# Score bursts held until due, half chunks as 32-row slices and lent weight buffers in a hand-scheduled attention and SiLU block

## The chip, the cores and the metric

The kernel runs on one core of a Trainium2 chip. A core has five engines with queues of their own: TensorE (PE; its weight loads are shown apart as PEld), VectorE (DVE), ScalarE (ACT), GpSimd (POOL) and SyncE (SP, which issues nearly all DMAs here). The metric is the device time of one execution in microseconds, as the median of several runs. Times inside an execution come from one profiled execution, counted from its first instruction.

## The reference

A layer norm feeds multi-query attention (32 query heads of 20 columns, one key head, one value head) and a SiLU feed-forward block of width 1728; both are added to the input. S is 2048, D is 640, all in bfloat16.

```python
def _A_ref(x, wq, wk, wv, wo):
    q = (x @ wq).reshape(B, S, H, Dh).transpose(0, 2, 1, 3)
    k = x @ wk
    v = x @ wv
    scores = jnp.einsum("bhqd,bkd->bhqk", q, k) * (Dh ** -0.5)
    p = softmax(scores, axis=-1)
    o = jnp.einsum("bhqk,bkd->bhqd", p, v)
    return o.transpose(0, 2, 1, 3).reshape(B, S, H * Dh) @ wo
def _B_ref(x, w1, w2):
    return jnp.einsum("bsf,fd->bsd", silu(jnp.einsum("bsd,df->bsf", x, w1)), w2)
x = A_x
xn = layernorm(x)
return x + _A_ref(xn, A_wq, A_wk, A_wv, A_wo) + _B_ref(xn, B_w1, B_w2)
```

## The kernel before

Queries are cut into four chunks (QC) of 512 rows, heads into eight groups (NG) of four, so there are 32 head groups with 16 key tiles and four heads each: 2048 score blocks of 128 keys by 512 queries. A head has 20 columns padded to 32, so a score matmul uses 32 of TensorE's 128 rows, and up to four of them with different row groups run beside each other: a score burst. A value matmul uses 32 of the 128 columns and four of them make a quad; the weight products (projections, feed-forward, output) are cut into quads of the same kind. Going from bursts to quads or back is a switch of TensorE's tile shape.

There are eight PSUM banks. Bank 7 (UB) collects the value products of a group, the other seven hold scores and weight products in turn. A score block takes one of two ways:

- ScalarE takes the exponential of a set of two or three banks in one instruction (line 1140 of the kernel before).
- VectorE turns single banks into integers whose bits read as bfloat16 approximate the exponential (line 1336, "p1", into a z buffer, four heads to a batch). From each batch two shifted copies are made, on GpSimd (line 1375) or on VectorE (line 1380), and all three go through the value matmuls with different weights, so that the approximation's errors even out.

The order of the work is decided in Python when the kernel is built. A planner (class `Sched` and the loop at the end of `build`) keeps an estimated clock per engine, picks the next operation with `step_pe` or `step_other` and appends it to that engine's list; `emit` then writes the lists out with semaphore waits. On the chip each engine simply runs its list. `step_pe` collects candidates: "s" a score burst for ScalarE (`make_s_act`), "d" a score block for VectorE, "p" and "pd" value quads, "m" and "l" quads of weight products, "r" a 32-row slice of a weight chunk. It takes the first kind that can start, in an order that depends on TensorE's present shape. `row_slice` lets a whole weight chunk of 128 rows be done as four matmuls of 32 rows, each in a free row group of a score burst (issued by `row_mm`, line 441); `col_mm` (line 434) issues chunks as quads.

The constants of these choices are in `BASE`; the letters of `PLAN` name a rule out of `RULES` for each 10 us of planned time. `stay` is such a constant: if it is not 0, and TensorE is not in burst shape, and ScalarE has work in hand for longer than `stay` plus 230 ns, score bursts go nearly to the end of the order. `claim` opens VectorE's batches in z buffers that are idle; there are five, two of which share memory with a staging area of wq.

The feed-forward width 1728 is thirteen chunks of 128 rows and one of 64. The half chunks of two neighbouring query chunks are computed together (`h_pair`): the even one's 64 rows lie in the upper half of its chunk and the odd one's in the lower half, and the rest is zero. `ffn_mms` lists the fourteen chunks of an output tile in order. The output of the first three query chunks is made by `out_job`, that of the last one by `y_job` (feed-forward and the packs known so far), and `fin_job` with the last heads' part.

After the last exponential come, on TensorE, the last value quads, the row sums of the last group ("sum", line 973), the spread of their reciprocals (line 991) and the final chunks; VectorE adds them up (line 941) and two queues store the result. ScalarE copies the last value bank out in two halves (line 1237) ahead of the sums. Other lines that the text uses: 756 is the tanh of the SiLU, 618 a copy of the keys, 52 and 2 tanh instructions stand at lines 756 and 728, line 1648 is a filler matmul on zeros that the planner puts into gaps.

Of the kernel before, what the change touches and what calls it, by code (L numbers as in the profile page):

```python
# [14 lines left out]
P = 128  # L15
# [81 lines left out]
BASE = dict(hold2=0, bnd=4, pj=6000.0, rows=0, rowmin=3, lagmax=6, lagp=0, lagj=6, openlag=5, late=-0.02, lead=0.01, leadmax=0.02, need=460.0, hold=300.0, dwant=600.0, slack=550.0, dnow=400.0, hungry=0.0, patience=0.0, keep=460.0, open=2, zcap=9, stay=0.0, homes=1, want=1, claim=6)  # L97
RULES = dict(a={}, b=dict(keep=0.0), c=dict(lagp=3), d=dict(lagp=5), e=dict(lagp=0), f=dict(patience=200.0), g=dict(dwant=0.0),
             h=dict(zcap=4), i=dict(zcap=3), j=dict(homes=0), k=dict(leadmax=-1.0, lead=-1.0), l=dict(lead=0.08, leadmax=0.1),
             m=dict(need=560.0), n=dict(hold=0.0), o=dict(stay=460.0), p=dict(open=1), q=dict(slack=400.0), r=dict(hungry=1000.0), s=dict(claim=9), t=dict(open=3), u=dict(claim=4), v=dict(want=2), w=dict(slack=700.0), x=dict(hold2=4), y=dict(bnd=0), z=dict(pj=-1e9), A=dict(rows=0), B=dict(rows=2, rowmin=2), C=dict(pj=2000.0), D=dict(openlag=3), E=dict(pj=8000.0), F=dict(hold2=3), G=dict(rows=1))  # L100
PLAN = "aaanGtxBBExhEhmxadrBBzraCBBEGqtrztfFzrqhwnpofocotyxddmGjvmpBaBitntqo"
# [17 lines left out]
class Op:  # L119
    __slots__ = ("eng", "fn", "occ", "lat", "pre", "reads", "writes", "prio", "mode", "slots",  # L120
                 "start", "fin", "done", "deps", "inc", "job", "first", "last", "gate", "on_commit", "seq", "name",
                 "dma_sem", "dma_val", "port", "run", "cut", "ends", "sync")

    def __init__(self, eng, fn, occ, lat=0.0, pre=(), reads=(), writes=(), prio=5.0, mode=None, slots=None,
                 job=None, gate=None, on_commit=None, name=""):
        self.eng = eng
        self.fn = fn
        self.occ = occ
        self.lat = lat
        self.pre = list(pre)  # L130
        self.reads = list(reads)
        self.writes = list(writes)
        self.prio = prio
        self.mode = mode
# [12 lines left out]
        self.port = False  # L147
        self.cut = None
        self.sync = None
        self.ends = (True, True)  # L150
# [168 lines left out]
def build(nc, A_x, A_wq, A_wk, A_wv, A_wo, B_x, B_w1, B_w2, out, stack):  # L319
# [78 lines left out]
    z_t += [zx[:, i * HG * QW:(i + 1) * HG * QW] for i in range(2)]  # L398
    wq_st = zx[:, 0:DC * D].rearrange("p (c d) -> p c d", c=DC)
# [266 lines left out]
    def q_job(qc, k):  # L666
# [11 lines left out]
        xq_read[qc].append(job)  # L678
        op = Op("dve", lambda v: v.tensor_scalar_mul(q_st[:, st, :], bk(job.bank), QSCALE), t_dve(512), 140,  # L679
# [26 lines left out]
    xq_read = {k: [] for k in range(QC)}  # L706
    t_users = {}
    out_done = {}

    def h_pair(qb):  # L710
# [13 lines left out]
        for q in (qa, qb):  # L724
            xq_read[q].append(job.ops[-1])
        ts = (qb * FC + fk) % 2
# [16 lines left out]
    def h_job(qc, fk):  # L743
# [9 lines left out]
        xq_read[qc].append(job)  # L753
        ts = (qc * FC + fk) % 2
# [134 lines left out]
    def y_job(qc, i, hf):  # L889
        e0, e1 = hf * HALF, (hf + 1) * HALF  # L890
        mms = ffn_mms(qc, i, e0, e1, True, not YC[i]) + o_mms(qc, i, e0, e1, False, True, range(YC[i]))
        job = pe_job(f"y{qc}_{i}_{hf}", mms, (14 + YC[i]) * 140, dyn=True)
        op = Op("dve", lambda v: v.scalar_tensor_tensor(out=yx[:, i, e0:e1], in0=bk(job.bank, 0, HALF), scalar=0.5,  # L893
# [114 lines left out]
    att = {"sgroup": 0, "pgroup": 0, "n": 0, "items": 0, "value": 0.0}  # L1008
# [248 lines left out]

    def z_idle(k):
        b = z_last[k]
# [57 lines left out]
    def yx_users(zi):  # L1317
        return [wqp0] if zi >= NZ0 else []
# [213 lines left out]
    def ready_to_make(m):  # L1532
# [11 lines left out]
        if m[0] == "y":  # L1544
            if (m[1], m[2]) not in xres_op or any((m[1], fk) not in hc_op for fk in range(FC)):
                return False
            return all((m[1] - 1, t) in out_done for t in range(QTP)) and all((m[1], g) in pack_op for g in range((YC[m[2]] * P - 1) // (HG * DH) + 1))
# [105 lines left out]
    def pe_candidates():  # L1653
# [11 lines left out]
        lead = misc_done[0] / misc_total - PACE * prog - ENDLEAD * max(0.0, prog - ENDFROM) / (1.0 - ENDFROM)  # L1665
        behind = lead < ru.lead or recent() < BUSY
# [28 lines left out]
    def row_slice(piece):  # L1695

        job = piece.job
        if not job.dyn or not ru.rows or sc.pe_mode != "s" or sc.pe_set is None or sc.t["pe"] > sc.pe_set[2] + 1.0 or job.burst == sc.pe_set[0]:
            return None
        busy = sc.pe_set[1]  # L1700
        pick = next(((x, r) for x in job.rest for r in job.rest[x] if r not in busy), None)
        if pick is None and len(job.rest) < ru.rows and len(piece.mms) > ru.rowmin:
            x = next((x for x in list(piece.mms)[-2:0:-1] if x.cut is not None and all(p.done for p in x.pre)), None)
# [53 lines left out]
    def step_pe():  # L1757
# [34 lines left out]
        elif mode == "p":  # L1792
            order += ["p", "pd", "m", "d", "l"] if lag >= (ru.lagp if cur_job[0] is None else ru.lagj) else ["m", "pd", "p", "d", "l"]
# [35 lines left out]
    def commit_pe(e, op, what):  # L1829
# [244 lines left out]
```

## Time and profile before

| | |
|---|---|
| time, median of 3 runs | 693.72 us (693.70 to 693.74) |
| the profiled execution's own time | 693.9 us |
| its span, first to last instruction | 692.1 us |
| granted TensorE clock | 1.000 |
| busy on TensorE, ScalarE, GpSimd, VectorE | 680.5, 673.5, 593.0, 572.0 us |
| weight loads on TensorE | 229.7 us |
| chain that ended last | ScalarE 57%, TensorE 35%, VectorE 5%, GpSimd 3% |

In a row of groups stand the line, the engine and operation, what it writes and reads, the shapes and the count; then busy time and the mean duration in ns, and the engine's idle time before these instructions with what ended it. Rows of a timeline begin with the start and the length of a run of equal instructions, in us. Records of following instructions on one engine can overlap, since each lasts until its result has landed.

### The profile page before, as it was taken

To read this page: it belongs to the slowest core of one execution; us is meant where nothing else is said; L and a number is where in the kernel's file an instruction comes from. 1 tells how busy PE (TensorE), PEld (TensorE's weight loads), DVE (VectorE), ACT (ScalarE), POOL (GpSimd) and SP (SyncE) were. 2 spreads that over 40 slices of the span, in tenths; PEclk is the share of its full clock that TensorE was granted. 3 is DMA by queue.
4 is the path that set the end of the run, shared out by engine and by line. 5 is a ranking of instruction groups with operands and counts; after the bars stand their busy time and mean duration, and the time that the engine had idled before them with its cause. 6 is when DMAs were issued, how large, how long until landed. Compare 5 with 4: busy or idle time off the path is not lost.

```text
span 692.1 us, 22655 instructions
## 1 busy us (share of the span) xinstructions
PE 680.5 (98%) x9908; PEld 229.7 (33%) x9911; DVE 572.0 (83%) x977; ACT 673.5 (97%) x727; POOL 593.0 (86%) x355
## 2 busy tenths in 40 slices
PE   8999999999999999999999999999999999999998
PEld 5432222222222333322223333322222333333344
DVE  7788889988988788789989878789898877888843
ACT  6899999999999999999999999999999999999993
POOL 6658999899988789898998879989889999988890
PEclk9999999999999999999999999999999999999999
DMA  8642220222221222233202222122222202232201
GB/s 223 194 158 39 20 22 14 35 33 27 22 19 14 37 39 24 29 74 35 27 9 28 31 29 33 22 63 41 30 20 21 22 19 31 31 68 23 23 7 40
DMA packets 34241, 28.97 MB, mean 42 GB/s; under 512 B 15486, under 2 KB 29662, under 8 KB 34142
## 3 DMA queue, kind: packets, MB, share of 16 engines
q1 hardware_dynamic: 33854, 27.20, 25.5%
q8 instruction: 77, 1.26, 0.7%
q10 hardware_dynamic: 288, 0.33, 0.1%
q14 instruction: 22, 0.18, 0.1%
HBM read 11.09 MB, written 2.62 MB: 20 GB/s over the span
## 4 chain that ended last, share of the span: by engine, by line
ACT 57%; PE 35%; DVE 5%; POOL 3%; issue 1%; DMA 0%
ACT sbt L1140 53%; PE psall L434 11%; PE psall L1175 11%; PE psall L1052 11%; ACT sbt L756 3%; POOL sbt L1375 2%; DVE sbt L1336 1%; DVE sbt L552 1%; DVE sbt L550 1%; DVE sbt L594 1%; POOL sbt L836 0%; DMA sbt<-in_A_x_dram 0%; PE psall L608 0%; PE psall L973 0%; DVE sbt L679 0%
## 5 line engine op out<-in xcount | busy, mean ns | idle before, releaser
L1140 ACT ACTIVATE sbt<-psall 128x1024 bf16<-128x1024 f32 (+1 forms) x655 | 652.5, 1220 | 2.2 <-PE psall L1052 1.7
L1375 POOL TENSOR_SCALAR sbt<-sbt 128x2048 int16<-128x2048 int16 x279 | 530.5, 1901 | 62.7 <-DVE sbt L1380 12.7
L1336 DVE TENSOR_SCALAR sbt<-psall 128x512 int16<-128x512 f32 x656 | 428.8, 684 | 79.6 <-PE psall L1052 72.0
L1052 PE MATMUL psall<-sbt 32*128 32x512 bf16 x2048 | 265.9, 384 | 3.7 <-ACT sbt L1140 1.8
L1175 PE MATMUL psall<-sbt 128*32 128x512 bf16 x3360 | 267.7, 384 | 1.2 <-DVE sbt L1223 0.4
L434 PE MATMUL psall<-sbt 128*32 128x320 bf16 (+2 forms) x3844 | 226.6, 331 | 0.7 <-ACT sbt L1140 0.5
L1052 PEld LDWEIGHTS psall<-sbt 32*128 32x128 bf16 x2048 | 70.0, 91 | 248.8 <-ACT sbt L1140 194.9
L434 PEld LDWEIGHTS psall<-sbt 128*32 128x32 bf16 x3844 | 83.9, 95 | 77.7 <-issue 46.9
L1175 PEld LDWEIGHTS psall<-sbt 128*32 128x32 bf16 x3360 | 66.0, 94 | 115.1 <-issue 82.4
L836 POOL TENSOR_TENSOR sbt<-sbt 128x512 bf16<-128x512 f32 x30 | 38.3, 1276 | 6.8 <-DVE sbt L1380 4.8
L759 DVE SCALAR_TENSOR_TENSOR sbt<-sbt,psall 128x512 bf16<-128x512 bf16 x52 | 35.5, 683 | 5.6 <-ACT sbt L756 4.9
L1380 DVE TENSOR_SCALAR sbt<-sbt 128x2048 int16<-128x2048 int16 x49 | 39.8, 827 | 0.2
L756 ACT ACTIVATE sbt<-psall 128x512 bf16<-128x512 f32 x52 | 39.5, 760 | 0.0
L1223 DVE COPY sbt<-psall 128x512 f32<-128x512 f32 x31 | 21.1, 682 | 2.3 <-PE psall L1175 2.2
L441 PE MATMUL psall<-sbt 32*128 32x320 bf16 (+1 forms) x60 | 20.5, 342 | 0.1
L1648 PE MATMUL psall<-sbt 128*32 128x256 bf16 (+1 forms) x264 | 18.1, 370 | 1.2 <-DVE sbt L474 1.2
L878 DVE SCALAR_TENSOR_TENSOR sbt<-psall,sbt 128x320 bf16<-128x320 f32 x24 | 11.6, 483 | 3.7 <-PE psall L434 2.6
L679 DVE TENSOR_SCALAR sbt<-psall 128x512 bf16<-128x512 f32 x20 | 13.5, 674 | 0.1
L893 DVE SCALAR_TENSOR_TENSOR sbt<-psall,sbt 128x320 f32<-128x320 f32 x8 | 3.9, 485 | 9.8 <-PE psall L434 9.7
L572 POOL TENSOR_SCALAR sbt<-sbt 128x640 bf16<-128x640 bf16 x12 | 10.4, 878 | 1.5 <-DVE sbt L564 1.2
L559 POOL TENSOR_TENSOR sbt<-sbt 128x2 f32<-128x2 f32 x8 | 5.6, 695 | 6.4 <-DVE sbt L557 6.1
L1648 PEld LDWEIGHTS psall<-sbt 128*32 128x32 bf16 x264 | 7.3, 113 | 6.2 <-issue 3.4
(63 smaller groups left out, 111.9 us busy)
## 6 DMA issues: line engine op xcount, KB each, us to landing
sbt<-sbt SPq DMA_DIRECT2D x120, 64.0 KB, 3.8
sbt<-in_A_x_dram SPq DMA_DIRECT2D x28, 160.0 KB, 3.3
sbt<-sbt SPq DMA_DIRECT2D x213, 20.0 KB
out_dram<-sbt SPq DMA_DIRECT2D x14, 160.0 KB, 1.9
sbt<-in_B_w_dram SPq DMA_DIRECT2D x1, 2160.0 KB, 12.7
sbt<-in_B_w_dram SPq DMA_DIRECT2D x1, 2080.0 KB, 8.2
sbt<-sbt SPq DMA_DIRECT2D x75, 8.0 KB
sbt<-in_A_wq_dram SPq DMA_DIRECT2D x1, 800.0 KB, 6.8
```

The costliest lines, as they stand in the source:

```text
L434: ins = pe.matmul(ps[j * SLOT:(j + 1) * SLOT, b * BANK + off:b * BANK + off + n], w[:, j * SLOT:(j + 1) * SLOT], x, start=start, stop=stop ...
L756: t = Op("act", lambda a: a.activation(t_buf[0:rows, ts, :], bk(job.bank, 0, QW, rows=rows), AF.Tanh, scale=0.5), t_act(512), 215, pre=[jo ...
L759: u = Op("dve", lambda v: v.scalar_tensor_tensor(out=hT[par][0:rows, fk, :], in0=t_buf[0:rows, ts, :], scalar=1.0, in1=bk(job.bank, 0, QW, ...
L836: nm = pool(lambda e: e.tensor_tensor(oU[:, us, :], U_sb[:, us, :], Rrep, ALU.mult), 1356.0, pre=[uc] + lc + pack_op.get(divmod(g - 2, NG) ...
L1052: return pe.matmul(bk(b), kT_rep[i * SLOT:(i + 1) * SLOT, kt * P:(kt + 1) * P], qT[i * SLOT:(i + 1) * SLOT, g % NQ, :], start=True, stop=T ...
L1140: return a.activation(Ebuf[:, es * QW:es * QW + w], ps[:, buf[0] * BANK:buf[0] * BANK + w], AF.Exp, scale=ESCALE)
L1175: ins = pe.matmul(ps[i * SLOT:(i + 1) * SLOT, UB * BANK:UB * BANK + QW], lhsT, rhs, start=(first and k < HG), stop=(last and k >= len(lst) ...
L1223: uc = Op("dve", lambda v: v.tensor_copy(U_sb[:, us, :], bk(UB)), t_dve(512), 140, pre=[pv] + up, reads=[sc.banks[UB]], writes=[res("U", u ...
L1336: p1 = Op("dve", lambda v: v.tensor_scalar(z16[:, i * QW:(i + 1) * QW], bk(job.bank), ZBIAS, 0.0, ALU.add, ALU.max), t_dve(QW) + 2.0, 140, ...
L1375: op = pool(lambda v, t=t, j=j, zin=zin: v.tensor_scalar(t.bitcast(I16), zin, float(SHIFT[j]), 1.0, ALU.add, ALU.mult), POOL_SHIFT, 0.0, p ...
L1380: op = dve(lambda v, t=t, j=j, zin=zin: v.tensor_scalar_add(t.bitcast(I16), zin, float(SHIFT[j])), t_dve(N, 4), prio=SPRIO - 0.01 * j, **args)
L1648: ins = pe.matmul(ps[i * SLOT:(i + 1) * SLOT, UB * BANK:UB * BANK + n], zero_t[:, 0:SLOT], zero_t[:, 0:n], start=fresh, stop=fresh, tile_p ...
```

## The change

Five things change, and with the new rule string the planner lays out the whole order anew behind the opening. `stay` is 520 by default and rule o, which set it to 460, now sets it to 0; J and K set 440 and 600. `half` allows a half chunk to be done as two 32-row slices, only on the rows that hold its data, and `ffn_mms` lists it last but one so that it can be. Three more z buffers lie in wq's and w1's memory and may be used once the last projection that reads these weights is done. The y jobs' readiness asks for at most NG - 2 groups of packs. A further constant, `pace`, with `lagl` chooses another threshold for value quads when the lead of the weight products falls below it.

```diff
-BASE = dict(hold2=0, bnd=4, ..., stay=0.0, homes=1, want=1, claim=6)
+BASE = dict(pace=-1.0, lagl=3, half=6, hold2=0, bnd=4, ..., stay=520.0, homes=1, want=1, claim=6)
...
-             m=dict(need=560.0), n=dict(hold=0.0), o=dict(stay=460.0), ...
+             m=dict(need=560.0), n=dict(hold=0.0), o=dict(stay=0.0), ..., H=dict(half=0), I=dict(half=3), J=dict(stay=440.0), K=dict(stay=600.0))
-PLAN = "aaanGtxBBExhEhmxadrBBzraCBBEGqtrztfFzrqhwnpofocotyxddmGjvmpBaBitntqo"
+PLAN = "acaoGrrqhBxxfmqFEBhBahwyaawqByamzyExoawBhpawrBKxjKzCzoqrqfBKEmBttt"
...
+        self.rows = tuple(range(HG))
...
+    NZ1 = len(z_t)
+    z_t.append(wq_sb[:, :, :].rearrange("p c d -> p (c d)")[:, 0:HG * QW])
+    z_t += [w1f[:, QTP * D + 2 * P + k * HG * QW:QTP * D + 2 * P + (k + 1) * HG * QW] for k in range(2)]
...
+    def short(job, qc):
+
+        for op in job.ops:
+            if hc_op[(qc, FC - 1)] in op.pre and op.cut is not None:
+                op.rows = tuple(range(HG))[:HG // 2] if qc % 2 == 0 else tuple(range(HG))[HG // 2:]
+        return job
+
     def ffn_mms(qc, i, e0, e1, start, stop):
...
-        for fk in range(FC):
+        for fk in [*range(FC - 2), FC - 1, FC - 2]:
...
+        short(job, qc)
...
+    lent_z = {}
+    Z_LENT = {NZ1: ("q", QC * DC), NZ1 + 1: ("h", QC * FC), NZ1 + 2: ("h", QC * FC)}
+
     def z_idle(k):
+        if k in Z_LENT and k not in lent_z:
+            w, n = Z_LENT[k]
+            if len(w_read[w]) < n or not all(o.done for o in w_read[w]):
+                return False
+            lent_z[k] = sc.order["pe"][-1]
...
-            return ... and all((m[1], g) in pack_op for g in range((YC[m[2]] * P - 1) // (HG * DH) + 1))
+            return ... and all((m[1], g) in pack_op for g in range(min((YC[m[2]] * P - 1) // (HG * DH) + 1, NG - 2)))
...
+        if pick is None and not job.rest and len(piece.mms) > ru.half > 0:
+            x = next((x for x in list(piece.mms)[1:-1] if len(x.rows) < HG and all(p.done for p in x.pre)), None)
+            if x is not None:
+                pick = next(((x, r) for r in x.rows if r not in busy), None)
...
-            order += [...] if lag >= (ru.lagp if cur_job[0] is None else ru.lagj) else [...]
+            order += [...] if lag >= (ru.lagj if cur_job[0] is not None else ru.lagl if att["lead"] < ru.pace else ru.lagp) else [...]
...
-                job.rest[x] = list(range(HG))
+                job.rest[x] = list(x.rows)
```

More of the change, by code (lines that the diff above doesn't have):

```diff
@@ L1697, in row_slice @@
         job = piece.job
-        if not job.dyn or not ru.rows or sc.pe_mode != "s" or sc.pe_set is None or sc.t["pe"] > sc.pe_set[2] + 1.0 or job.burst == sc.pe_set[0]:
+        if not job.dyn or not (ru.rows or ru.half) or sc.pe_mode != "s" or sc.pe_set is None or sc.t["pe"] > sc.pe_set[2] + 1.0 or job.burst == sc.pe_set[0]:
             return None
@@ L1701, in row_slice @@
         pick = next(((x, r) for x in job.rest for r in job.rest[x] if r not in busy), None)
+        if pick is None and not job.rest and len(piece.mms) > ru.half > 0:
+            x = next((x for x in list(piece.mms)[1:-1] if len(x.rows) < HG and all(p.done for p in x.pre)), None)
+            if x is not None:
+                pick = next(((x, r) for r in x.rows if r not in busy), None)
         if pick is None and len(job.rest) < ru.rows and len(piece.mms) > ru.rowmin:
[L1703 removed]
+            x = next((x for x in list(piece.mms)[-2:0:-1] if x.cut is not None and len(x.rows) == HG and all(p.done for p in x.pre)), None)
             r = next((r for r in range(HG) if r not in busy), None)
@@ L1792, in step_pe @@
         elif mode == "p":
-            order += ["p", "pd", "m", "d", "l"] if lag >= (ru.lagp if cur_job[0] is None else ru.lagj) else ["m", "pd", "p", "d", "l"]
+            order += ["p", "pd", "m", "d", "l"] if lag >= (ru.lagj if cur_job[0] is not None else ru.lagl if att["lead"] < ru.pace else ru.lagp) else ["m", "pd", "p", "d", "l"]
         else:
```

18 lines of the change are left out of this document (12 added, 6 removed).

## The prediction

> **What bounds the kernel now.** I read the page's first table, then the sums by window, the groups by shape, the waits, the chain of waits, and last the timelines of ScalarE and TensorE where the kernel begins and ends. The page has two engines at the limit.
>
> ```profile
> PE 680.5 (98%) x9908; PEld 229.7 (33%) x9911; DVE 572.0 (83%) x977; ACT 673.5 (97%) x727; POOL 593.0 (86%) x355
> ```
>
> Which of the two sets the time? The windows (us, then busy time of PE, PEld, DVE, ACT, POOL) say ScalarE:
>
> ```profile
> 40.00:120.00 80.00, 78.79 (x1019) 22.55 (x1015) 69.94 (x113) 80.00 (x94) 72.64 (x40) 1.00 0.21 28
> 120.00:200.00 80.00, 78.97 (x1049) 22.88 (x1050) 72.23 (x116) 80.00 (x94) 72.73 (x40) 1.00 0.24 27
> ...
> 600.00:640.00 40.00, 39.98 (x643) 14.00 (x640) 33.73 (x55) 40.00 (x42) 35.96 (x21) 1.00 0.28 41
> 640.00:692.10 52.10, 48.74 (x906) 22.54 (x898) 28.98 (x49) 41.44 (x39) 31.37 (x19) 1.00 0.13 23
> ```
>
> ScalarE has 80.00 of 80.00 us in the middle. Its records overlap, so "busy" could hide small stalls; I therefore add up its work from the chain of waits, where back-to-back steps show the true price, and compare with the time it had.
>
> ```profile
> 509.54 3.67 ACT sbt L1140 x4
> 513.21 0.49 ACT sbt L756
> 513.70 4.58 ACT sbt L1140 x5
> 518.28 0.49 ACT sbt L756
> 518.77 4.10 ACT sbt L1140 x4
> ```
>
> Four two-bank exponentials take 3.67 us and five 4.58, so one is 0.917 us. The four at 518.77 hold one three-bank set: 4.10 - 3 x 0.917 = 1.35; other such rows give 1.34, which I use. A tanh is 0.49.
>
> ```profile
> L1140 ACT ACTIVATE sbt<-psall 128x1024 bf16<-128x1024 f32 x573 | 555.0, 1172 | 0.3
> L1375 POOL TENSOR_SCALAR sbt<-sbt 128x2048 int16<-128x2048 int16 x279 | 530.5, 1901 | 62.7 <-DVE sbt L1380 12.7 <-DVE sbt L1336 9.7 <-PE psall L1175 8.0
> L1336 DVE TENSOR_SCALAR sbt<-psall 128x512 int16<-128x512 f32 x656 | 428.8, 684 | 79.6 <-PE psall L1052 72.0 <-PE psall L441 3.0
> ...
> L1140 ACT ACTIVATE sbt<-psall 128x1536 bf16<-128x1536 f32 x82 | 124.6, 1555 | 1.9 <-PE psall L1052 1.7
> ...
> L1380 DVE TENSOR_SCALAR sbt<-sbt 128x2048 int16<-128x2048 int16 x49 | 39.8, 827 | 0.2
> ```
>
> ```profile
> 12.84 2.37 ACT L1140 ACTIVATE sbt<-psall 128x1536 bf16<-128x1536 f32 x2
> 15.60 4.62 ACT L1140 ACTIVATE sbt<-psall 128x1536 bf16<-128x1536 f32 x4 [0.40 <-PE psall L1052]
> 20.98 0.60 ACT L618 ACTIVATE sbt<-psall 128x512 bf16<-128x512 f32 x1 [0.76 <-PE psall L608]
> 22.08 6.89 ACT L1140 ACTIVATE sbt<-psall 128x1536 bf16<-128x1536 f32 x6 [0.49 <-PE psall L1052]
> ...
> 30.07 5.97 ACT L1140 ACTIVATE sbt<-psall 128x1536 bf16<-128x1536 f32 x5 [0.56 <-PE psall L1052]
> ...
> 658.75 22.15 ACT L1140 ACTIVATE sbt<-psall 128x1536 bf16<-128x1536 f32 x18
> 681.40 0.66 ACT L1237 ACTIVATE sbt<-psall 128x256 f32<-128x256 f32 x2 [0.50 <-PE psall L1175]
> ```
>
> From 12.84 to 680.90 (658.75 + 22.15) ScalarE had 668.1 us. Its work is 573 x 0.917 + 82 x 1.34 + 54 tanh x 0.49 + 3 copies of the same width x 0.49 = 525.4 + 109.9 + 26.5 + 1.5 = 663.3. Of the 4.8 us left, the rows above show 2.2 as waits before 31 us (0.40 + 0.76 + 0.49 + 0.56). So over the other 640 us it loses at most 2.6 us. The score loads, in turn, wait for it:
>
> ```profile
> PEld psall L1052 <- ACT sbt L1140: 194.9, 503, 0.8
> ...
> POOL sbt L1375 <- DVE sbt L1380: 12.7, 16, 1.3
> ```
>
> 503 times the weight load of a score burst stood until an exponential gave its banks back. The kernel is ScalarE's 12.84 us of start, 668.1 of work, and a tail of 692.1 - 680.9 = 11.2.
>
> [...]
>
> **The change part by part.** The built order of the changed program gives counts; all times are rows of before.
>
> *Exponentials.* It has 74 three-bank and 581 two-bank sets for 82 and 573: 8 x (1.34 - 0.917) = 3.4 us less on ScalarE. The 8 score blocks that left went to VectorE (664 for 656, two batches more). Up to the eighteenth set the PE and ScalarE orders are the same, so the start and its 2.2 us of waits stay.
>
> *Two more batches* cost VectorE 8 x 0.684 + 2 x 0.827 = 7.1 us and GpSimd 2 x 1.90 = 3.8. They lie beside ScalarE. Over the last eight of the 32 head groups VectorE gets 14 more blocks and 9 more shifts (17 us over some 165); in 120 to 200 it is already 72.23 of 80, and ScalarE lost nothing there. So I take zero; if that cover went, the 7.1 us would be the bound.
>
> [...]
>
> *Lent buffers* only add places for those batches; no copy is issued for them. Their first user waits for the last matmul that read the weights, late in the kernel. Zero.
>
> *Half chunk as slices, chunk order swapped.* 72 slices of 320 columns for 32, and 32 of 512 for 28, ride in score bursts; 320-column quads fall from 572 to 549. Prices from TensorE's timeline:
>
> ```profile
> 659.61 0.40 PE L1052 MATMUL psall<-sbt 32*128 32x512 bf16 x4
> 659.94 0.61 PE L1175 MATMUL psall<-sbt 128*32 128x512 bf16 x8
> 660.49 0.39 PE L1052 MATMUL psall<-sbt 32*128 32x512 bf16 x3
> 660.81 0.40 PE L1175 MATMUL psall<-sbt 128*32 128x512 bf16 x4
> ```
>
> A burst of four takes 0.33 to the next start, one of three 0.32, so a slice rides for about nothing. A 512-column quad is near 0.22 (two take 0.55 with a switch of some 0.11). A 320-column quad is 0.14 (eight fill 679.83 to 680.95 below). On TensorE: 23 x 0.14 = 3.2 less; four more value quads 0.9; three more bursts 0.7; one projection quad and six switches less, 0.9; six wide fillers less and one narrow more, 1.2. Sum -3.7, or -2.5 without fillers, which stand in idle time. In the middle this is beside ScalarE and I price it at zero there.
>
> *Held score bursts.* Rule o held them in before as well, in a few stretches; now they are held everywhere but under o. The new limit is 520 ns in the planner's time, so a burst leaves with less than the 0.917 us of one set in hand. An unheld burst that starts early saves nothing where ScalarE is never idle; a late one costs its lateness. Bounds: below, all 2.6 us of remaining loss goes; above, one set in forty late by one value quad, 16 x 0.22 = 3.5. I take -0.3: nearly no change, since ScalarE is saturated with and without holding. The pace term compares a lead with -1.0, which the lead (a share done minus a share due) does not reach; the relaxed test of y still needs five groups of packs, as before. Both zero.
>
> *The end.* Here the new order pays. TensorE in before:
>
> ```profile
> 678.60 0.39 PE L1052 MATMUL psall<-sbt 32*128 32x512 bf16 x3
> 678.92 0.86 PE L434 MATMUL psall<-sbt 128*32 128x320 bf16 x20
> 679.61 0.40 PE L1175 MATMUL psall<-sbt 128*32 128x512 bf16 x4
> 679.83 1.26 PE L434 MATMUL psall<-sbt 128*32 128x320 bf16 x32
> 680.95 0.40 PE L1175 MATMUL psall<-sbt 128*32 128x512 bf16 x4
> 681.18 0.94 PE L434 MATMUL psall<-sbt 128*32 128x320 bf16 x32
> 682.05 1.05 PE L973 MATMUL psall<-sbt 128*128 128x4 f32 x8
> 683.03 0.24 PE L434 MATMUL psall<-sbt 128*32 128x128 bf16 x4
> 683.10 1.05 PE L991 MATMUL psall<-sbt 128*32 128x128 f32 x32
> 683.97 4.82 PE L434 MATMUL psall<-sbt 128*32 128x384 bf16 x124
> ```
>
> The last value quad (680.95) starts as the last exponential ends; then come four y quads and four narrow ones, the sums (L973), one narrow quad, the spread (L991), the final chunks. In the changed order the last value quad is followed by eleven y quads, then the sums, then all seventeen quads of the last y job, and only then the spread; the five narrow quads stand behind it. TensorE keeps this order. Sums later by 0.23 + 11 x 0.14 - 1.10 = 0.7; spread later by a further 17 x 0.14 - 0.07 = 2.3; final chunks by 5 x 0.06 = 0.3 more. Together +3.3. Low bound 2.3, if everything but the seventeen quads hides behind the two copies of L1237; high 3.8, if TensorE comes late to its last value quad by a 512-column pair.
>
> *Sum* against the profiled execution (span 692.1; its own time 693.9, the median of the runs 693.72): -3.4 + 3.3 - 0.3 = -0.4. Forecast 693.72 - 0.4 = **693.3**: what ScalarE saves is spent after it has ended.
>
> **The rivals.** (1) TensorE sets the time, as its 98% suggests: then the end moves by its work, -2.5 to -3.7, to 690.0-691.2. For it: the quads left for the end show TensorE behind. Against: 503 waits of score loads for ScalarE. (2) ScalarE's last losses go and the end grows by the low bound only: -3.4 - 2.6 + 2.3 = -3.7, or with half of that loss won and the end as summed -3.4 - 1.3 + 3.3 = -1.4: 690.0 to 692.3. For: 23 fewer quads and six fewer switches ahead of score bursts. Against: there are only 2.6 us to win. (3) Slower: holding starves ScalarE. Each held burst that misses its due moment idles ScalarE at once, as sets run back to back. It decides from 1.8 us of added loss, 2.8 ns a set; at one late set in forty the time is 693.72 - 0.1 + 3.5 = 697.1, at half of that 695.4. For: less in hand, and near the end the order has 41 and then 11 two-bank sets in a row with one three-bank set between, which need a burst every 0.917 us. Against: ScalarE's loss is already nearly nothing, so most bursts have room. [...]
>
> **How the numbers follow.** Forecast 0.53 (its own range 692.0 to 694.9); rival one 0.10, two 0.13, three 0.19, four 0.05. A measurement of this kernel tells 0.2%, 1.4 us, from no change. Faster (below 692.3): rivals one and two and the forecast's low edge, 0.24. Slower (above 695.1): rivals three and four, 0.24. The same: 0.52. Range 690.9 to 695.9: it leaves out the far parts of rivals one and two below and of three and four above, about 0.1 each.
>
> **What would show it.** ScalarE's last exponential ends at 677 to 678 instead of 680.9, at 80.00 of 80.00 in the middle; the tail from there grows from 11.2 to 14 or 15 us, with the y quads between sums and spread. A last exponential after 679.5 speaks for rival three; gaps of ScalarE released by score bursts would be its mark. A tail under 13.5 us makes the end's term wrong; an end earlier by more than 2 us with unchanged ScalarE prices makes the bound wrong.

## The result and the profile after

| | before | changed |
|---|---|---|
| median (12 runs each, side by side) | 693.87 us | 695.04 us |
| range of the runs | 693.62 to 694.66 | 694.80 to 697.08 |
| ratio | | 1.0020, 95% interval 1.0011 to 1.0029 |
| profiled execution, its own time and span | 693.9, 692.1 | 697.08, 695.3 (the longest of the twelve) |
| profiled again in the first experiment | | 695.11, 693.3 |

The change costs 1.2 us. The direction was forecast wrongly (693.3), and the time lies inside the range. Of the two profiles of the changed kernel the second is the ordinary one, and the rows below are of it unless they are said to be of the longest execution. First the engine row of the longest execution's page:

```profile
PE 678.7 (98%) x9852; PEld 228.4 (33%) x9855; DVE 577.1 (83%) x987; ACT 671.7 (97%) x727; POOL 595.8 (86%) x357
```

The shares are those of before and tell nothing of the 1.2 us. A window of the same execution (us, then busy PE, PEld, DVE, ACT, POOL):

```profile
40.00:120.00 80.00, 78.08 (x989) 22.88 (x986) 73.26 (x117) 79.52 (x93) 71.33 (x39) 1.00 0.21 28
```

The same window in the ordinary execution:

```profile
40.00:120.00 80.00, 79.26 (x1008) 22.78 (x1008) 72.92 (x119) 80.00 (x94) 72.21 (x40) 1.00 0.21 29
```

ScalarE has its 80.00 of 80.00 again, so the idle time of this stretch is one execution's own and no part of the 1.2 us. What recurs is at the back. The groups by shape, and ScalarE's timeline (start and length of a run of instructions; in brackets the idle time before it and what ended that):

```profile
L1157 ACT ACTIVATE sbt<-psall 128x1024 bf16<-128x1024 f32 x581 | 566.3, 1195 | 1.1 <-PE psall L1069 0.7
L1157 ACT ACTIVATE sbt<-psall 128x1536 bf16<-128x1536 f32 x74 | 113.8, 1583 | 1.7 <-PE psall L1069 1.5
...
L1361 DVE TENSOR_SCALAR sbt<-psall 128x512 int16<-128x512 f32 x664 | 436.0, 685 | 83.4 <-PE psall L1069 76.9 <-PE psall L445 2.3
```

```profile
535.36 0.81 ACT L735 ACTIVATE sbt<-psall 128x512 bf16<-128x512 f32 x1
535.84 17.82 ACT L1157 ACTIVATE sbt<-psall 128x1024 bf16<-128x1024 f32 x19
553.92 112.64 ACT L1157 ACTIVATE sbt<-psall 128x1024 bf16<-128x1024 f32 x117 [0.27 <-PE psall L1069]
667.01 11.83 ACT L1157 ACTIVATE sbt<-psall 128x1024 bf16<-128x1024 f32 x10 [0.44 <-PE psall L1069]
679.34 0.66 ACT L1254 ACTIVATE sbt<-psall 128x256 f32<-128x256 f32 x2 [0.50 <-PE psall L1192]
```

The last exponential ends at 667.01 + 11.83 = 678.84, 2.05 us earlier than before (680.90 in the prediction). The tail is 693.3 - 678.84 = 14.5 us for 11.2.

How much does ScalarE lose on the way there? The last tanh ends at 535.36 + 0.81 = 536.17, so the 146 sets behind it have 142.7 us. The groups of that window:

```profile
L1157 ACT ACTIVATE sbt<-psall 128x1024 bf16<-128x1024 f32 x131 | 123.1, 1103 | 1.1 <-PE psall L1069 0.7
L1157 ACT ACTIVATE sbt<-psall 128x1536 bf16<-128x1536 f32 x15 | 21.7, 1502 | 0.1
```

At the prediction's prices they are 131 x 0.917 + 15 x 1.34 = 140.2, and 2.4 us are lost. The same stretch of the kernel before:

```profile
536.04 0.71 ACT L728 ACTIVATE sbt<-psall 128x512 bf16<-128x512 f32 x1
536.51 12.09 ACT L1140 ACTIVATE sbt<-psall 128x1024 bf16<-128x1024 f32 x12
548.80 132.09 ACT L1140 ACTIVATE sbt<-psall 128x1536 bf16<-128x1536 f32 x128 [0.20 <-PE psall L1052]
```

There 140 sets, 35 of them of three banks by the groups of that window, have 680.89 - 536.75 = 144.1 us for 105 x 0.917 + 35 x 1.34 = 143.2: 0.95 lost. (The idle time in the rows is smaller, 1.2 and 0.2 us, since records overlap: a two-bank one lasts 1.10 and 1.11 us on the mean, at a price of 0.917. The end-to-end sum shows all of it.) Below, "late loss" is this quantity, from the last tanh to the last exponential.

Over the whole, from the first exponential at 13.17, ScalarE had 665.7 us for 581 x 0.917 + 74 x 1.34 + 57 x 0.49 = 659.9: a loss of 5.8 us for the 4.8 of before.

TensorE at the end, in the ordinary execution:

```profile
678.89 0.40 PE L1192 MATMUL psall<-sbt 128*32 128x512 bf16 x4
679.12 1.67 PE L438 MATMUL psall<-sbt 128*32 128x320 bf16 x44
680.72 1.06 PE L990 MATMUL psall<-sbt 128*128 128x4 f32 x8
681.70 2.49 PE L438 MATMUL psall<-sbt 128*32 128x320 bf16 x68
684.02 1.04 PE L1008 MATMUL psall<-sbt 128*32 128x128 f32 x32
684.89 5.10 PE L438 MATMUL psall<-sbt 128*32 128x128 bf16 x144
```

This is the order that the prediction read: last value quad, eleven y quads (x44), the sums, seventeen y quads (x68), the spread, the final chunks, with next to no idle time between.

### The profile page after: what moved, and what is told of

Read it like the earlier page. It is cut to its first block, busy times and chain, and to the rows that moved or that the text cites. A ratio compares the mean times of both kernels' runs of the same rounds, so it can differ in the third digit from the quotient of the medians.

```text
span 695.3 us, 22540 instructions
## 1 busy us (share of the span) xinstructions
PE 678.7 (98%) x9852; PEld 228.4 (33%) x9855; DVE 577.1 (83%) x987; ACT 671.7 (97%) x727; POOL 595.8 (86%) x357
## 3 DMA queue, kind: packets, MB, share of 16 engines
q8 instruction: 77, 1.26, 0.8%
## 4 chain that ended last, share of the span: by engine, by line
ACT 47%; PE 41%; DVE 7%; POOL 2%; DMA 1%; SPq 0%; issue 0%; POOLq 0%
ACT sbt L1157 44%; PE psall L1069 13%; PE psall L1192 13%; PE psall L438 13%; DVE sbt L1361 3%; ACT sbt L764 3%; POOL sbt L1400 1%; DVE sbt L1405 1%; DMA sbt<-sbt 1%; DVE sbt L556 1%; DVE sbt L554 1%; PE psall L586 0%; DMA sbt<-in_A_x_dram 0%; DVE sbt L598 0%; POOL sbt L851 0%
## 5 line engine op out<-in xcount | busy, mean ns | idle before, releaser
L1361 DVE TENSOR_SCALAR sbt<-psall 128x512 int16<-128x512 f32 x664 | 436.0, 685 | 83.3 <-PE psall L1069 76.5
L1192 PE MATMUL psall<-sbt 128*32 128x512 bf16 x3376 | 267.2, 384 | 3.2 <-POOL sbt L1400 1.2
L438 PE MATMUL psall<-sbt 128*32 128x320 bf16 (+3 forms) x3748 | 227.2, 332 | 0.7 <-ACT sbt L1157 0.2
L1069 PEld LDWEIGHTS psall<-sbt 32*128 32x128 bf16 x2048 | 71.2, 91 | 248.8 <-ACT sbt L1157 177.7
L438 PEld LDWEIGHTS psall<-sbt 128*32 128x32 bf16 x3748 | 80.7, 95 | 79.7 <-issue 50.6
L1192 PEld LDWEIGHTS psall<-sbt 128*32 128x32 bf16 x3376 | 68.1, 94 | 115.7 <-issue 77.5
L445 PE MATMUL psall<-sbt 32*128 32x320 bf16 (+1 forms) x104 | 34.3, 330 | 0.5
L1673 PE MATMUL psall<-sbt 128*32 128x256 bf16 (+1 forms) x244 | 15.3, 354 | 1.2 <-DVE sbt L478 1.2
L894 DVE SCALAR_TENSOR_TENSOR sbt<-psall,sbt 128x320 bf16<-128x320 f32 x24 | 11.5, 480 | 1.1 <-PE psall L1069 1.0
L445 PEld LDWEIGHTS psall<-sbt 32*128 32x128 bf16 x104 | 9.5, 91 | 2.3 <-PE psall L445 1.7
```

Of the source, the lines that this page charges most:

```text
L438: ins = pe.matmul(ps[j * SLOT:(j + 1) * SLOT, b * BANK + off:b * BANK + off + n], w[:, j * SLOT:(j + 1) * SLOT], x, start=start, stop=stop ...
L445: return pe.matmul(ps[0:w.shape[-1], b * BANK:b * BANK + n], w[k], x[k], start=start, stop=stop, tile_position=(r * SLOT, 0))
L1069: return pe.matmul(bk(b), kT_rep[i * SLOT:(i + 1) * SLOT, kt * P:(kt + 1) * P], qT[i * SLOT:(i + 1) * SLOT, g % NQ, :], start=True, stop=T ...
L1192: ins = pe.matmul(ps[i * SLOT:(i + 1) * SLOT, UB * BANK:UB * BANK + QW], lhsT, rhs, start=(first and k < HG), stop=(last and k >= len(lst) ...
L1361: p1 = Op("dve", lambda v: v.tensor_scalar(z16[:, i * QW:(i + 1) * QW], bk(job.bank), ZBIAS, 0.0, ALU.add, ALU.max), t_dve(QW) + 2.0, 140, ...
```

## The experiments

**The changed kernel once more**, as the base of the others.

> The changed kernel once more, for a profile of an ordinary execution: the one shown took 697.1 us where its median was 695.0. Theory A (ScalarE loses time because TensorE stands in its fixed order behind value quads and banks that GpSimd's and VectorE's late work releases) expects the last exponential to end at 678 to 680.9 with TensorE's waits for VectorE and GpSimd above the 1.2 us of before, and a tail of 14.5 us. Theory B (holding the score bursts starves ScalarE) expects the late bursts to stand behind work that ran without waits. Theory C (nothing but late DMA landings in the one execution shown) expects the last exponential at 677.5 or earlier.

695.13 us, ratio 1.0016 (1.0007 to 1.0025). The losses of the first 200 us are as in the kernel before and those past 536 us are all there, so nothing of the median is C's. (It fits the longest execution, which loses 2.1 us between 40 and 200 us for 0.05 here, and whose GpSimd waits 2.3 us for two DMAs for 0.2 here; that the one makes the other is not shown.) One of the recurring gaps, at 667 us, on the timeline of all engines:

```profile
663.66 2.90 ACT L1157 ACTIVATE sbt<-psall 128x1024 bf16<-128x1024 f32 x3
...
665.12 1.13 PE L438 MATMUL psall<-sbt 128*32 128x320 bf16 x28
665.51 0.68 DVE L1240 COPY sbt<-psall 128x512 f32<-128x512 f32 x1
...
666.25 0.40 PE L1192 MATMUL psall<-sbt 128*32 128x512 bf16 x4
...
666.58 0.43 PE L1069 MATMUL psall<-sbt 32*128 32x512 bf16 x4
```

The second of the three exponentials ends at 666.56 - 0.92 = 665.64 and frees banks for the burst. TensorE is in seven y quads then; behind them stands the first value quad of the next head group, which needs VectorE's copy of the last one (done at 666.19). The burst comes at 666.58, 0.9 us after its banks were free, and ScalarE loses 0.55 us.

**Shorter GpSimd shifts**, in the changed kernel and, as a control, in the one before. The shift covers two of the four heads; the value products of the other two read the unshifted z.

```diff
-v.tensor_scalar(t.bitcast(I16), zin, float(SHIFT[j]), ...)
+v.tensor_scalar(cut(t.bitcast(I16)), cut(zin), float(SHIFT[j]), ...)   # cut: first half
```

> The changed kernel in the same order, with GpSimd's shifted copies made of two heads of the four; the other two heads' value products read the unshifted buffer, so the output is not the reference's. GpSimd's shift falls from 1.90 us to about 1 us. Theory A expects ScalarE's loss in the middle to fall to that of before or lower: last exponential at 676.5 to 678, time 692 to 693.3. Theory B expects no more than 0.4 us less than the changed kernel, 694.6 to 695.1. Theory C expects a profile like an ordinary execution of the changed kernel.

> The kernel before with the same shortening of GpSimd's copies, as the control: it leaves out the same part of the computation. ScalarE loses at most 2.6 us there. Theory A expects 0.3 to 1.5 us less than before, less than what the changed kernel gains. Theory B expects the same small gain in both kernels.

694.08 us (ratio 0.9999, 0.9990 to 1.0008) for the changed kernel and 693.46 (0.9993, 0.9983 to 1.0002) for the one before: about 1.0 and 0.5 us less than with whole shifts. The first lies between the ranges of A and B. Shifts that others wait for are a part of the loss in both. With every one of them halved, the difference between the two kernels is 0.6 us instead of 1.2 (with intervals of 0.6 us each way on either, a rough figure), and the gap at 667 us stays. In the traces the late loss falls from 2.4 to 1.6 and from 0.95 to 0.5, so 1.1 of the 1.5 by which the two differ is left. So late shifts are not the whole answer.

**Score bursts moved ahead of quads.** 23 bursts that had work directly in front, and banks free by the planner's own clock, go up to four places earlier.

```diff
+if j < k and ...:
+    pe[j:e] = block + pe[j:k]     # block: the burst and what rides in it
```

> The changed kernel with the holding undone after planning: wherever the planner had a score burst's banks ready before the quads directly in front of it began, the burst is moved ahead of them (23 bursts, up to four quads each); all else in the order stays. Theory B expects 0.8 to 1.5 us less than the changed kernel: 693.5 to 694.2. Theory A expects 0 to 0.5 us less, since 23 bursts of 655 can't carry the loss and TensorE would still wait behind late copies: 694.5 to 695.1.

695.16 us, ratio 1.0013 (1.0005 to 1.0022): nothing, so this gives no support to B. It does show something at 667 us. The burst came almost a microsecond earlier, at 665.59, and its exponential hardly did:

```profile
665.59 0.39 PE L1069 MATMUL psall<-sbt 32*128 32x512 bf16 x2
...
666.32 0.39 PE L1192 MATMUL psall<-sbt 128*32 128x512 bf16 x4
...
666.76 1.94 ACT L1157 ACTIVATE sbt<-psall 128x1024 bf16<-128x1024 f32 x2 [0.40 <-PE psall L1192]
```

What releases the exponential now is the value quad (L1192): it reads the slot of the exponentials' buffer that this one is to write. The scores were there; the place for the result was not.

**The value quad and the burst put first**, alone and with VectorE's copy put first too: the question that the row above leaves.

```diff
+pe[i - 3:i + 2] = pe[i:i + 2] + pe[i - 3:i]     # i: the first value quad of the last group; then burst 645
...
+dv[i - 1:i + 1] = [dv[i], dv[i - 1]]            # i: VectorE's copy; only in the second kernel
```

> The changed kernel with the first value quad of the last head group and the score burst behind it (burst 645) put ahead of the last three of the seven y quads that stand in front of them; VectorE's order unchanged. In the changed kernel the exponential of this burst starts at 667.01, 0.55 us late; in the run with 23 bursts moved, the burst alone came at 665.59 and the exponential still only at 666.76, behind the value quad at 666.32. Theory V: the quad frees the slot of the exponentials' buffer that this exponential writes, and it waits for VectorE's copy of the value bank (665.51 to 666.19, behind a block of VectorE's own). Then this move alone wins little: TensorE stands until 666.2, the exponential starts 0.40 to 0.55 us late as before. Theory P: the three quads are what the burst waits for, and the gap falls by their 0.4 us to 0.1 to 0.2 us. The time is 694.6 to 695.2 by either.

> The same with VectorE's copy of the value bank put ahead of the block that stood before it (it could start at 664.9 instead of 665.51). Theory V: the copy is done by 665.6, the value quad and the burst follow at once, and the exponential starts 0 to 0.15 us late where it was 0.55; the last exponential ends 0.4 to 0.55 us earlier than 678.84 unless the block put back makes a later burst wait; 694.5 to 694.8 us. Theory P: no better than the run beside it.

With the move alone, TensorE stands for the copy and the gap stays to the hundredth (TensorE, then ScalarE):

```profile
666.16 0.40 PE L1192 MATMUL psall<-sbt 128*32 128x512 bf16 x4 [0.40 <-DVE sbt L1240]
...
666.92 1.94 ACT L1157 ACTIVATE sbt<-psall 128x1024 bf16<-128x1024 f32 x2 [0.44 <-PE psall L1069]
```

With the copy first as well, the gap is gone, eight sets run through, and a new one opens behind them:

```profile
661.07 7.44 ACT L1157 ACTIVATE sbt<-psall 128x1024 bf16<-128x1024 f32 x8
669.16 10.00 ACT L1157 ACTIVATE sbt<-psall 128x1536 bf16<-128x1536 f32 x8 [0.64 <-PE psall L1069]
```

Theory V holds for this gap: it waits for VectorE's copy, which stands behind a block of its own. The times are 695.84 us (ratio 1.0030, 1.0017 to 1.0042) and 695.46 (1.0022, 1.0012 to 1.0032), both above their expectation and neither better than the changed kernel. Bursts 645 and 646 stood side by side; three quads between them cost two more switches of the tile shape (some 0.11 us each, the prediction's estimate from its rows), and the next burst comes late in both kernels (gaps of 0.68 and 0.64 us). One gap is closed and the work that was put back opens the next.

**The quads of the tail left out.**

```diff
+elif op.name in ("y3_3_0", "y3_3_1") and not any(op.ends) and op.start > 678000.0 ...:
+    pass
```

> The changed kernel, with 25 of the y quads that its order places after the last exponential left out (10 of the eleven quads in front of the last four sums, and 15 of the 17 quads between the sums and the spread, each 4 matmuls); the places that they feed get incomplete sums, nothing else differs. Two theories of the tail. T1, the prediction's own: the tail is 3.3 us longer than before because TensorE has these quads to do there, at 2.49 us for 68 matmuls and 1.67 us for 44. Then the tail falls from 14.5 us by up to 3.8 us (25 quads of 0.146 us would be 3.7), and the kernel takes 691.4 to 692.2 us. T2: the chain sums, reciprocals, spread, normalising is as long by itself, and the quads only fill its waits. Then the tail falls by less than 1 us: 694.2 to 695.1 us. The ScalarE losses before the last exponential stay at 5.5 to 6 us by both.

692.23 us, ratio 0.9972 (0.9962 to 0.9983). ScalarE's last run and TensorE's end:

```profile
667.20 11.83 ACT L1157 ACTIVATE sbt<-psall 128x1024 bf16<-128x1024 f32 x10 [0.44 <-PE psall L1069]
```

```profile
679.08 0.40 PE L1192 MATMUL psall<-sbt 128*32 128x512 bf16 x4
679.31 0.31 PE L438 MATMUL psall<-sbt 128*32 128x320 bf16 x4
679.97 1.05 PE L990 MATMUL psall<-sbt 128*128 128x4 f32 x8 [0.35 <-ACT sbt L1254]
```

The tail is 690.5 - 679.03 = 11.5 us, 3.0 shorter, and the gap at 667 us is unchanged. T1 holds: the quads are the tail's growth. Of the 3.7 us of work 0.7 is not won, half of it the wait of the sums for ScalarE's copy (0.35) that the quads had covered.

**The late quads left out**, in the changed kernel and in the one before.

```diff
+elif op.name[:5] in ("out2_", "y3_0_", "y3_1_", "y3_2_") and not any(op.ends) ...:
+    pass
```

> The changed kernel with 199 quads left out: the inner quads of the out jobs of the third query chunk and of the first three y row tiles, which lie between 538 and 667 us in its order; their outputs are incomplete, the order of all that is left is the same. Theory A: from 520 us on ScalarE's losses (2.8 us in the trace of the changed kernel's second profile) are score bursts whose banks are ready 0.5 to 0.9 us before TensorE comes to them through the quads in front. Then these losses fall to under 0.8 us and the last exponential ends 2.0 to 2.8 us earlier, at 676.0 to 676.8; the tail stays at 14.5 us; 692.3 to 693.1 us in all. Theory B: the bursts are held back by the rule and by banks that other engines empty late, and the quads only fill the time. Then the losses stay above 2 us and the time at 694.4 to 695.2.

> The control of the run before it: the kernel before the change, with the same kind of quads left out (210, between 540 and 665 us). Its losses from 520 us on are 0.9 us, so by theory A it gains 0.5 to 0.9 us (693.0 to 693.5), and the difference between the two kernels shrinks from +1.1 to about -0.6 us; by theory B both gain about the same and the difference stays at about +1.1 us.

705.13 us (ratio 1.0155) and 707.07 (1.0185): both far slower with less to do, which neither theory had. The windows of the first, where the leaving out begins (the column after POOL is the granted TensorE clock):

```profile
538.00:540.00 2.00, 1.48 (x19) 0.41 (x16) 1.78 (x3) 2.00 (x3) 1.92 (x2) 1.00 0.04 10
540.00:542.00 2.00, 1.61 (x18) 0.40 (x14) 1.55 (x3) 2.00 (x4) 1.92 (x2) 1.00 0.14 34
542.00:544.00 2.00, 1.38 (x17) 0.34 (x14) 1.83 (x4) 2.00 (x4) 1.92 (x2) 0.61 0.02 5
544.00:546.00 2.00, 2.00 (x20) 0.31 (x12) 1.79 (x4) 1.77 (x3) 1.92 (x2) 0.50 0.05 8
```

TensorE is busy for 1.48 and 1.61 of 2 us, ScalarE still without a gap; then the clock falls to half, and on the half clock TensorE is busy throughout and ScalarE starves (1.77). The pair decides nothing between A and B.

**A quarter of the late quads left out**, every fourth, so that TensorE stays busier.

```diff
+elif op.name[:5] in ("out2_", "y3_0_", "y3_1_", "y3_2_") and op.seq % 4 == 0 ...:
+    pass
```

> The changed kernel with 51 of the 199 late quads left out, about every fourth, spread from 538 to 667 us (the run without all 199 gave ScalarE larger losses, with a granted clock of 0.74 to 0.91 in five of its stretches past 540 us, and so did not decide). Theory A, TensorE's work in front of the bursts is what ScalarE waits for past 520 us: its losses there fall from 2.8 us to 0.6 to 1.6, the granted clock stays at 1.00, and the kernel takes 693.4 to 694.4 us. Theory B, banks and holding: the losses stay at 2.4 to 3.0 and the time at 694.8 to 695.4. Theory C: any idle TensorE time in this part lowers the granted clock: it falls below 0.95 in at least one stretch of 20 us, and the kernel takes 696 us or more.

694.49 us, ratio 1.0012 (1.0002 to 1.0021), 0.5 to 0.6 less than the changed kernel, just above A's range and below B's. Two windows:

```profile
540.00:560.00 20.00, 19.37 (x290) 6.28 (x287) 18.57 (x31) 19.67 (x22) 18.89 (x13) 1.00 0.23 27
...
600.00:620.00 20.00, 19.83 (x298) 6.35 (x299) 17.98 (x30) 20.00 (x22) 17.35 (x10) 1.00 0.32 57
```

Its ScalarE:

```profile
535.15 0.81 ACT L735 ACTIVATE sbt<-psall 128x512 bf16<-128x512 f32 x1
...
553.71 112.30 ACT L1157 ACTIVATE sbt<-psall 128x1024 bf16<-128x1024 f32 x117 [0.33 <-PE psall L1069]
666.27 11.86 ACT L1157 ACTIVATE sbt<-psall 128x1024 bf16<-128x1024 f32 x10 [0.26 <-PE psall L1069]
```

The clock stays at 1.00. The same 146 sets end at 678.13, with a late loss of 678.13 - 535.96 - 140.2 = 1.9 us for 2.4; the gap at 667 us is 0.26 for 0.44, the one at 554 us is no smaller. C is out. A has a part, behind 600 us more than ahead of it, but not the 1.2 to 2.2 that it had claimed. (The expectations say 2.8 us; counted from end to end, as here, it is 2.4.)

**The last letters of the rule string altered**, in the changed kernel and, as a control, in the one before. Up to some 610 us all is unchanged; a letter further ahead that differs in the control too left its order as it was up to there.

```diff
-PLAN = "acaoGrrqhBxxfmqFEBhBahwyaawqByamzyExoawBhpawrBKxjKzCzoqrqfBKEmBttt"
+PLAN = "acaoGrrqhBxxfmqFEBhBahwyaawqByamzyExoawBhpawrBKxjKzCzoqrqfBKEmppttt"
...
-PLAN = "...mxadrBBzraCBBEGqtrztfFzrqhwnpofocotyxddmGjvmpBaBitntqo"
+PLAN = "...mxvdrBBzraCBBEGqtrztfFzrqhwnpofocotyxddmGjvmpBasitntyy"
```

> The changed kernel with its rule string altered from the 63rd letter on (...BKEmBttt becomes ...BKEmppttt); its order is the same up to 623 us, and past that it has 1 y quad after the last exponential where the changed kernel has 31, and 12 more of its sets are of three banks. Theory: the changed kernel is lost in its last 70 us only, as the place of the last y quads and the bursts that wait behind quads there. Then the last exponential ends later (by the sets of three banks up to 0.04 us each is lost, and by the quads done before it up to 3 us) but the tail comes down to 11 to 12 us, and the whole to 693.4 to 694.4 us, below the changed kernel by 0.7 us or more. If it stays at 695.0 or above, moving the quads ahead of the last exponential costs ScalarE as much as they cost in the tail, and the place of the quads isn't what the change lost by.

> The control of the run with altered last rules: the kernel before the change, with its own string altered in the same way (its order is the same up to 612 us; past that no y quad is left after the last exponential, where it had 6, and 6 more of its sets are of three banks). If the changed kernel's late part was merely badly placed, with more to gain there than the kernel before, this gains less than the 1.25 us that the changed kernel gained: 0 to 0.6 us, 693.4 to 694.0, and the two kernels end level. If it gains as much, 692.6 to 693.0, the change as such costs its 1.1 us with either string.

The changed kernel takes 693.84 us (ratio 0.9996, 0.9987 to 1.0005), 1.2 less than with its own string; the one before 693.78 (0.9995, 0.9986 to 1.0004), 0.2 less. They end level. ScalarE and TensorE of the first:

```profile
535.41 0.81 ACT L735 ACTIVATE sbt<-psall 128x512 bf16<-128x512 f32 x1
...
576.86 104.27 ACT L1157 ACTIVATE sbt<-psall 128x1024 bf16<-128x1024 f32 x101 [0.15 <-PE psall L1069]
```

```profile
681.28 0.40 PE L1192 MATMUL psall<-sbt 128*32 128x512 bf16 x4
...
682.38 1.05 PE L990 MATMUL psall<-sbt 128*128 128x4 f32 x8
...
683.53 1.05 PE L1008 MATMUL psall<-sbt 128*32 128x128 f32 x32
```

No gap from 576.86 on: the 667 us one is gone. With 567 two-bank and 86 three-bank sets ScalarE has (567 - 581) x 0.917 + (86 - 74) x 1.34 = +3.2 us more to do. The late loss is 681.13 - 536.22 - (117 x 0.917 + 27 x 1.34) = 1.4 for 2.4. By stretches, from end to end of the exponentials, all that went lies past 640 us: 0.04 there for 1.1 in the changed kernel (0.3 in the one before). From 537 to 600 us both orders of the changed code lose 1.2, the kernel before 0.7. The last exponential is 2.3 us later (681.13), the tail 3.6 shorter (692.0 - 681.13 = 10.9). So work moved between ScalarE and the tail is nearly an even trade in this direction too, and most of the gain of the whole is the loss of 1.0 that went.

**Six named bursts put first**, in the kernel with the altered string: those that were late in the trace, not in the planner's clock.

```diff
+for n, k in ((254, 2), (257, 1), (383, 1), (552, 2), (553, 1), (582, 1)):
+    pe[i - k:j] = pe[i:j] + pe[i - k:i]
```

> The kernel of the run with altered last rules (693.84 us there, against 694.07 before), with six score bursts put in front of the one or two pieces of TensorE work that stood directly ahead of them (bursts 254, 257, 383, 552, 553 and 582, which in the profile of the changed kernel find their banks ready 0.48 to 0.62 us before TensorE comes to them, and cost ScalarE 0.10, 0.10, 0.13, 0.25, 0.15 and 0.13 us). Theory A, TensorE's fixed order: most of these 0.85 us goes, 0.4 to 0.8 us in all, and nothing comes in elsewhere: 693.0 to 693.5 us, faster than before by 0.1 to 0.15 per cent. Theory Q, TensorE as a queue: the work put back is late instead and the next bursts behind it lose the same, as in the run with 23 bursts moved; the losses stay within 0.2 us and the time at 693.6 to 694.1.

694.18 us, ratio 1.0004 (0.9995 to 1.0013). ScalarE around bursts 552 to 554:

```profile
578.00 1.02 ACT L1157 ACTIVATE sbt<-psall 128x1024 bf16<-128x1024 f32 x1 [0.65 <-PE psall L1069]
579.32 102.06 ACT L1157 ACTIVATE sbt<-psall 128x1536 bf16<-128x1536 f32 x99 [0.29 <-PE psall L1069]
```

```profile
577.58 0.39 PE L1069 MATMUL psall<-sbt 32*128 32x512 bf16 x3 [0.17 <-DVE sbt L894]
```

Burst 552 has no gap any more, and the next two have 0.65 and 0.29: burst 553 waits for VectorE to empty an output bank (L894), whose last quad was among what was put back. Theory Q holds. No version of either code beat the kernel before by more than the measurement tells.

**No lent buffers**, the string and all else kept.

```diff
+z_t = z_t[:NZ1]
```

> The changed kernel without the three lent buffers (nine buffers of bit patterns and two in the x buffer, as before), all else the same, the string too; the order differs from where the first lent buffer was taken. If the lent buffers carry the eight added VectorE columns' worth of batches, fewer batches fit in late, more sets go to ScalarE and the last exponential ends 3 to 6 us later than 678.8: 696 to 698 us. If they do little, 694.6 to 695.6 us.

696.64 to 697.97 us in four runs, ratio 1.0048 (1.0034 to 1.0061). VectorE and ScalarE:

```profile
L1362 DVE TENSOR_SCALAR sbt<-psall 128x512 int16<-128x512 f32 x652 | 429.2, 685 | 89.9 <-PE psall L1070 84.1 <-PE psall L446 2.3
```

```profile
609.35 74.80 ACT L1158 ACTIVATE sbt<-psall 128x1536 bf16<-128x1536 f32 x76 [1.25 <-PE psall L1070]
```

VectorE takes 652 blocks instead of 664, and the last exponential ends at 684.15, 5.3 us later. The buffers do carry batches. The sets alone (573 of two banks, 83 of three, one of one bank) are 5.2 us more work for ScalarE. Since the string was chosen for the code with the buffers, this prices the part under a string that doesn't fit, no more.

## Why the prediction was wrong

- **Bound.** Right: 51 quads less on TensorE in the late part (some 7 us at 0.14) moved the end by 0.6 only. (That start, ScalarE's time and tail add up to the span holds in any run, with the losses as the remainder; it is no test.) Rival one (690.0 to 691.2) is out.
- **Exponentials, -3.4.** Right: the counts are 581 and 74 and their prices the same.
- **The end, +3.3.** Right: 14.5 for 11.2, and leaving its quads out takes 3.0 back.
- **Two more batches, lent buffers: zero.** The buffers carry batches, as said. Rival four (0.05) had GpSimd or VectorE late with these batches: the 3.8 us of GpSimd's work and 1.7 us of waits for the two VectorE shifts, 5.5 in all. No run shows the 1.7; the size is out, as the kernel is only 1.2 us slower. But zero was too kind. GpSimd's waits for VectorE's shifts are 21.4 us in 22 waits for 12.7 in 16, 8.7 more where two more shifts at the mean of before (12.7 / 49 each) make 0.5; how much of that reached ScalarE no run separates. Halved shifts win 1.0 us for 0.5 in the kernel before, though the intervals are too wide to tell these apart. And the largest gap waits for a VectorE copy behind a block. Slack over a stretch of 80 us doesn't say that the one instruction that is waited for comes in time.
- **Held bursts, -0.3: here it failed.** "I take -0.3: nearly no change, since ScalarE is saturated with and without holding." ScalarE's loss grew by 1.0 us over the whole (the late loss by 1.5, while 0.5 ahead of it went, 0.3 of that between 40 and 520 us). So the term held in the middle and failed past 536 us. The step read the saturation as a sign of slack. At 80.00 of 80.00 ScalarE has no slack to give, and the prediction had itself found what uses it up: 41 and 11 two-bank sets in a row that need a burst every 0.917 us, more VectorE blocks in the last groups, y quads pushed to the back. It gave the first to rival three, at 0.19, priced the second at zero and the third in the tail alone. The last exponential came at 678.84, later than the 677 to 678 that the forecast named and earlier than the 679.5 that it left to rival three. That rival's mark (gaps released by score bursts) came, below its 1.8 us; its stated cause did not show, since bursts moved forward won nothing. Whether holding as such has a part in the 1.0 us is not shown. The mark was badly chosen: "released by a burst" looks the same whether the burst was held, stood behind quads, or stood behind a value quad that waits for VectorE.
- **The rest of the difference.** From 693.3 to 695.04 are 1.74 us: 1.3 is this term, 0.3 a later start (first exponentials at 13.17 for 12.84, before any order differs; in the run without the tail's quads it is 12.88, with 0.4 us more lost before 40 us, so this split is one execution's), 0.15 the kernel before, at 693.87 beside the changed one for 693.72.

What is shown: -3.4 and +3.3 cancel, and the kernel is slower by ScalarE's late gaps; another order of the last 70 us takes 1.0 us of them away, all past 640 us, and the two kernels end level. The largest gap hangs on VectorE's copy, and where it was closed, or a burst put forward, the next gap opened. What stays open: how the 1.2 us between 550 and 580 us divide between VectorE and TensorE, and what holding does alone, which wasn't tried, since without it the same string lays out another order.

## What to carry to other kernels

Here two engines stood at 97% and 98%, each with a fixed list, and of 3.4 us taken from the one 1.0 came back as gaps late in the list, between 550 and 580 us and past 640. With such a pair, price lateness where the list is densest, not by the mean slack. Add up end to end (time had, minus count times back-to-back price): overlapping records hid half of the loss here (1.2 of 2.4 us). And when work is moved behind the last step of the bounding engine, count it in the tail at its full price; that half of the sum was exact.

## What the runs showed of the hardware

Less TensorE work made the kernel 10 us slower (705.13 us for 695.13). In the run with 199 quads left out the granted clock fell to 0.50 after some 4 us at about 77% busy ((1.48 + 1.61) of 4 us), though its waits for ScalarE were all short:

```profile
PE psall L1069 <- ACT sbt L1157: 18.3, 52, 0.7
```

52 waits in the execution, the longest 0.7 us; in these 4 us TensorE's idle time came in short gaps, the longest 0.52 us. Between 550 and 554 us it was busy for 1.53 and 1.47 of 2 us, as little as ahead of the fall, and the clock was 1.00 there; so these rows give no busy share at which it falls. In the control the clock was 0.83 between 540 and 560 us, with 16.49 of 20 us busy, for 1.00 and 19.90 in the 20 us ahead. With a quarter of the quads left out TensorE was busy for 19.4 us and more of 20, and the clock stayed at 1.00. An ablation that removes matmuls has to look at the granted clock before its time is read.

In a run of ScalarE's records without a gap the starts were closer together than the ends. The kernel before, just ahead of the stretch of the chain that the prediction reads:

```profile
504.16 3.98 ACT L1140 ACTIVATE sbt<-psall 128x1024 bf16<-128x1024 f32 x4
507.77 0.85 ACT L756 ACTIVATE sbt<-psall 128x512 bf16<-128x512 f32 x1
```

By their starts four exponentials take 507.77 - 504.16 = 3.61 us, by the chain, which goes from end to end (504.47 to 508.13), 3.67. Each record here is some 0.013 us longer than the one ahead of it (1.23 us the first, 1.26 the fourth). The value quad that waits for the last exponential of the kernel before starts at 680.95, 0.05 us after that record's end (680.90). So a price and a loss have to be taken from the same side; in this text both go by ends.
